# A DeltaNet and SwiGLU kernel's prologue: beta through TensorE, L in three operations, conversions after the rounds

## Chip, cores, metric

One core of a Trainium2 chip runs the whole program. The metric is device time of one execution in microseconds (us). Engine names as the profile has them: PE is TensorE (PEld its weight loads), DVE is VectorE, ACT is ScalarE, POOL is GpSimd, SP is SyncE, which here only issues DMAs.

## The reference

Two blocks follow each other, all in float32. The first is a gated linear attention with a delta rule, for 4 batches and 8 heads, 768 steps, head size 48:

```python
k_n = k / (np.linalg.norm(k, axis=-1, keepdims=True) + 1e-06)
for t in range(S):
    y[t] = q[t] @ state
    v_old = state.T @ k_n[t]
    state = state + beta[t] * outer(k_n[t], v[t] - v_old)
```

Its output, as 3072 tokens of 384 features, goes through a feed-forward block with d_ff 1536: `(silu(x @ w_gate) * (x @ w_val)) @ w_out`.

## The kernel before

The attention is done in chunks of 64 steps (12 chunks; c is the chunk). In a chunk, the recurrence becomes a triangular system: K times K transposed (the "gram"), scaled by beta and by the norms of K, is inverted, and the inverse is multiplied with V. PE does the products; DVE does the substitution, since it is a chain of small steps. Two chunks form a group g, and 32 heads of batch and head lie side by side in the tiles. The feed-forward products of a chunk (lines L1093, L1189, L1216, L1299) fill PE between the attention's steps, and they make up most of the time.

The order of the instructions on each engine is written out by hand (a manual schedule): each engine works its own queue strictly in that order, and waits by semaphore for what an instruction needs. The change touches only the start of the program, before PE has feed-forward work. In that start, in order:

- SP and ACT each issue one half of the loads of chunk 0's K, then of chunk 1's (`load_k`, L135). Rows of 48 floats make many small packets. Then 16 small loads of beta (`load_beta`, L387) go out, alternately from POOL and from SP or ACT; each brings eight rows for one block of 32 steps, so that beta arrives in the layout in which it is used. SP goes on with Q of chunk 0, K of 2 and 3, Q of 1, V and the weights (`stage`, L253).
- `unread` (L582): 100 small products on PE whose result nobody reads, before K has landed.
- `norms` (L363, L371) on DVE: squares of K and their sums; the square root on POOL (L375).
- `turned` (L444): eight transposes on PE per K or Q, copied out by ACT (L446). K has 16 heads in two banks of one PSUM tile, called p_t.
- `first_gram` (L592, L593) for chunks 0 and 1: for every head two products, one for the upper ("hi") 32 steps with 32 columns, one for the lower ("lo") 32 steps with 64 columns. `first_diag` (L598) copies the diagonal blocks out, one half by ACT, one by DVE. ACT copies beta to `beta_b` (L1573). DVE turns the blocks (L1577), scales them (L621), and `first_substitution` (L637, L643) does 15 steps of inversion for 16 by 16 blocks. `first_z` turns the result back, and `spread_z` (L656, L658) writes it to `ztp`.
- `low_copies` (L605, L610) on ACT: the parts L of the gram below the diagonal blocks, in six operations per chunk, three per half of the partitions.
- Q's and later K's transposes, and the grams of chunks 2 and 3 and of Q with K (`gram_steps`, L458), on PE behind that.
- `n_products` (L667): L times the block inverse, on PE; then `advance(0)`, which holds a short series: the product p_u (L876), and three rounds of two half rounds each, a product on PE (L896) and an addition on DVE (`plus`, L1260). Then p_y, the copies y, the transposes to `x_ffn` (L989, L992), and the first gate product (L1189).

The weights come as float32 and are split into parts by `power_step` on ACT (L265, L271) and `convert` on DVE (L282, L290, L302), piece by piece. Pieces 0, 2, 4 are the first columns of the gate weights; 1, 3, 5 of the value weights. Before, one conversion stands behind each half round of chunk 0:

```python
        for n in (0, 2, 4, 1, 3, 5):
            step("advance", advance, 0)
            converts_first(n)
```

Of the kernel before, what the change touches and what calls it, by code (L numbers as in the profile page):

```python
# [8 lines left out]
FP32 = mybir.dt.float32  # L9
# [4 lines left out]
C = 64  # L14
DP = 64
R = 32
# [4 lines left out]
def kernel(  # L21
# [25 lines left out]
    nc = tc.nc  # L47

    B, H, S, D = q.shape
# [63 lines left out]
    ident = const.tile([128, 128], FP32, name="ident")  # L113
    nc.gpsimd.memset(knp[0][:, :, :, D:DP], 0.0)
    make_identity(nc, ident)
    for t in knp[1:] + qpad:
        nc.gpsimd.memset(t[:, :, :, D:DP], 0.0)
    ZB = 2
    ztp = [const.tile([128, 2, HH, C], FP32, name=f"zt{i}") for i in range(ZB)]
# [103 lines left out]
    place_of += [("z1", H_ * n) for n in (2, 3, 1, 0)]  # L223
    place_of += in_wo + in_work + (in_z1 + in_work) * 3

    beta_s = places["wo"].bitcast(FP32)[:, 6 * H_ : 6 * H_ + NG * 128]
    LATE = {"zb": 18, "p_sb": 12}
    freed_by = {}
    for n, (name, lo) in enumerate(place_of):
# [27 lines left out]
    def power_step(n):  # L257
        if n in powers or n not in staged:
            return
        dst, _, t, f0, m = pieces[n]  # L260
        power = words(hp[10 + (n // 2 % 4 if n < N_HALF else (0, 2, 3, 1)[(n + 2) % 4])])
        power = power[:, n % 2 * m : n % 2 * m + m] if n < N_HALF else power[:, 0:m]
        powers[n] = power
        words_of = staged[n].rearrange("p (f two) -> p f two", two=2)
        nc.scalar.activation(  # L265
            dst[:, t, f0 : f0 + m],
            words_of[:, :, 1].bitcast(FP32),
            ACTF.Copy,
            scale=2.0**-112,
        )  # L270
        nc.scalar.activation(power, words_of[:, :, 0], ACTF.Copy, scale=2.0**-29)  # L271
# [75 lines left out]
    def every():  # L347
        for bp in range(NB):
            for j in range(NJ):
                for n, (par, b) in enumerate(ORDER):  # L350
                    yield bp, j, par, b, bp == 0 and j == 0
# [28 lines left out]
                out=beta_b[:, g], in0=beta_b[:, g], in1=r_n, op=ALU.mult  # L380
            )

    def load_beta(at, queue=nc.gpsimd):

        s_, blk, c, par = at // 8, at // 4 % 2, at // 2 % 2, at % 2
        lo, m = 64 * c + R * blk, (NG - 1) * 128 + R
        queue.dma_start(  # L387
            out=beta_s[8 * at : 8 * at + 8, 0:m],
            in_=beta.rearrange("(b bp) (j par) s -> b par bp j s", b=2, par=2)[
                s_ ^ par, par, :, :, lo : lo + m  # L390
            ],
        )

    def first_n():
        n = n_t[0].rearrange("p c h -> p (c h)")
# [17 lines left out]
    def banks(name, tag):  # L413

        if type(tag) is int:
            return [ps_ffn([128, 512], name, tag + i) for i in range(2)]
        p = ps_pair(name, tag)
        return [p[:, 0], p[:, 1]]

    def turned(c, of_q, tag=None):  # L420

        if tag is None:
            tag = "py" if of_q else "px"
        x = qpad[c % QB] if of_q else kn_of(c)
        if of_q:
            xt = work.tile([128, NB * NJ * 2 * C], FP32, name="qt", bufs=1)
        else:
            xt = kt_of(c)
        if c >= blocks_of[of_q][1]:
            xt_v = xt.rearrange("p (b bp j i) -> p bp j b i", bp=NB, b=2, j=NJ)  # L430
            (qt if of_q else kt)[c] = xt_v
            blocks = blocks_of[of_q][2]
            nc.vector.transpose(xt, blocks.rearrange("p bp h d -> p (bp h d)"))
            spent.append(1.8)
            if c + 1 < NCH:
                late_loads.append(lambda: load_blocks(of_q, c + 1))
            return
        xt = xt.rearrange("p (bp j b i) -> p bp j b i", bp=NB, j=NJ, b=2)
        (qt if of_q else kt)[c] = xt
        p_t = banks("p_t", tag)  # L440
        for bp in range(NB):
            for j in range(NJ):
                at = slice(128 * j, 128 * j + 128)
                nc.tensor.transpose(p_t[bp][:, at], x[:, bp, 2 * j : 2 * j + 2], ident)  # L444
        for bp in range(NB):
            nc.scalar.copy(xt[:, bp].rearrange("p j b i -> p (j b i)"), p_t[bp])  # L446
        if of_q and c + QB < Q_BLOCKS:
            load_q(c + QB)
# [104 lines left out]
    def first_tiles():  # L553
        a = work.tile([128, C * 2 * HH], FP32, name="a_sb")
        for c in range(2):
            l_sb[c] = a[:, R * R * c : R * R * (c + 1)].rearrange(
                "p (h k) -> p h k", k=C
            )
        first_of["flat"] = new_mb().rearrange("p k i -> p (k i)")
        first_of["diag"] = first_of["flat"].rearrange("p (j h) -> p h j", j=R)  # L560
        first_of["zb"] = places["z1"].bitcast(FP32)[:, 4 * H_ - 1056 : 4 * H_]
        first_of["mb"] = places["wo"].bitcast(FP32)[:, 2 * H_ : 2 * H_ + 1056]
        nc.vector.memset(first_of["zb"], 0.0)
        nc.vector.memset(a, 0.0)
        for x, rows in enumerate((slice(16, C), slice(R, C), slice(48, C), slice(0, R))):
            nc.vector.tensor_reduce(
                out=m_two[:, x],
                in_=ident.rearrange("p (b n) -> p b n", b=2)[:, :, rows],
                axis=mybir.AxisListType.X,
                op=ALU.add,  # L570
            )
        nc.vector.tensor_tensor(
            out=m_rows, in0=m_two[:, :, 0], in1=m_two[:, :, 1], op=ALU.add
        )
        nc.vector.tensor_scalar_mul(m_low, m_rows[:, 0:3], -1.0)

    def unread():

        p = ps_pair("p_t", "px")[:, 0]
        for n in range(100):  # L580
            q_ = QUADS[n % 4][0]
            nc.tensor.matmul(p[q_, 0:1], ident[q_, q_], ident[q_, 0:1])  # L582

    def first_gram(c, tag):

        p_g = ps_pair("p_g", tag)
        p_v = p_g.rearrange("p par (x h i) -> p par x h i", x=2, i=R)
        for bp, j, par, b, _ in every():
            k_v = kt[c][half_of(par), bp, j, b].rearrange("p (x i) -> p x i", x=2)
            h, s_ = NJ * bp + j, b ^ par  # L590
            hi, lo = slice(64 * s_, 64 * s_ + R), slice(64 * s_ + R, 64 * s_ + C)
            nc.tensor.matmul(p_v[hi, par, 1, h], k_v[:, 0], k_v[:, 0])  # L592
            nc.tensor.matmul(p_v[lo, par, :, h], k_v[:, 1], k_v)  # L593
        return p_v

# [3 lines left out]

    def low_copies(c, p):  # L600
        l_v = l_sb[c].rearrange("p (par h) k -> p par h k", par=2)
        for s_ in range(2):
            hi, lo = QUADS[2 * s_][0], QUADS[2 * s_ + 1][0]
            for rows, x in ((hi, 0), (lo, 2)):
                nc.scalar.mul(  # L605
                    l_v[rows, :, :, B16 * x : B16 * x + B16],
                    p[rows, :, 1, :, 0:B16],
                    m_low[rows, x : x + 1],
                )
            nc.scalar.mul(l_v[lo, :, :, 0:R], p[lo, :, 0], -1.0)  # L610

    def first_scale(r_b):
        zb, b = first_of["zb"], beta_b[:, 0]
# [46 lines left out]
    def n_products(c, p_n, pars):  # L660

        zt = ztp[0][:, c]
        p_v = [p.rearrange("p (bp j i) -> p bp j i", bp=NB, j=NJ) for p in p_n]
        for bp, j, par, b, _ in every():
            if par in pars:
                rows, h = half_of(b ^ par), HH // 2 * par + NJ * bp + j
                nc.tensor.matmul(  # L667
                    p_v[par][half_of(b), bp, j], l_sb[c][rows, h], zt[rows, h]
                )
# [732 lines left out]
    def converts_first(*ns):  # L1402

        convert(list(ns), 0)
        for n in ns:
            todo.remove(n)
# [132 lines left out]
    with tc.manual_schedule(  # L1539
# [6 lines left out]
        }  # L1546
    ):
        new_n(0)
        for at in range(0, 16, 2):
            load_beta(at)  # L1550
            load_beta(at + 1, nc.sync if at % 4 else nc.scalar)
        first_tiles()
        norms(0)

        norms(1)
        load_q(0)
        load_k(2)
# [8 lines left out]
        copy_a, copy_v = nc.scalar.copy, nc.vector.tensor_copy  # L1566
        unread()
        turned(0, False)
        turned(1, False, "py")
        p_g = [first_gram(0, "px"), first_gram(1, "py")]  # L1570
        first_diag(0, 0, p_g[0], copy_a)
        first_diag(0, 1, p_g[0], copy_v)
        copy_a(beta_b, beta_s.rearrange("p (g r) -> p g r", g=NG)[:, :, 0:R])  # L1573
        first_diag(1, 0, p_g[1], copy_a)
        r_b = first_n()
        first_diag(1, 1, p_g[1], copy_v)
# [32 lines left out]
        power_step(2)  # L1609
        for x in range(2):  # L1610
            spread_z(1, x, nc.scalar)
            power_step((4, 1)[x])
        power_step(3)
        power_step(5)
        for n in (0, 2, 4, 1, 3, 5):
            step("advance", advance, 0)
            converts_first(n)
        step("advance", advance, 0)
        p_n = banks("p_n", "px")
        n_products(1, p_n, (0,))  # L1620
        step("advance", advance, 0)
        n_products(1, p_n, (1,))
        scale_v(1)
        for par in range(2):
            n_copy(1, p_n, par)
# [73 lines left out]
```

## Time and profile before

| | |
|---|---|
| median of 3 runs | 711.52 us (709.63 to 712.78) |
| the profiled execution | 709.14 us |
| its span, first to last instruction | 707.4 us |
| PE busy | 683.2 us, 97% of the span |
| PEld busy | 643.0 us, 91% |
| DVE busy | 473.6 us, 67% |
| ACT busy | 261.8 us, 37% |
| POOL busy | 52.9 us, 7% |
| mean granted clock of PE | 0.992 |

The shares are averages over very different stretches. In the page's slices, each character is one fortieth of the span (17.7 us) and gives the busy tenths; the first three slices are the start that the change touches. A row of the order of time reads: start, duration, engine, line, operation, output and inputs, shapes, count, and in brackets the idle time before and what ended it. "issue" stands for waiting for nothing that the profile shows. A row of the chain reads start, duration, what; a row of the waits reads who waited for whom, the sum, how often, the longest.

### The profile page before, as it was taken

What the parts mean: (1) busy time and instruction counts of PE and PEld (TensorE: products, weight loads), DVE (VectorE), ACT (ScalarE), POOL (GpSimd) and SP (SyncE); (2) the same over time, 40 slices, a digit from 0 to 9 for tenths busy, and PEclk for the clock granted to TensorE, in tenths of its full rate; (3) what the DMA queues carried; (4) which work ended last, traced back from release to release, by engine and by line L of the source; (5) the groups of instructions that cost most, each with busy time, mean ns of one, the idle gap of its engine ahead of it and who ended that gap; (6) DMA issues with size and microseconds to landing.
All of it is one profiled execution on the core that took longest, in us unless ns stands there. A gap on an engine that the chain in (4) does not pass through costs nothing.

```text
span 707.4 us, 25711 instructions
## 1 busy us (share of the span) xinstructions
PE 683.2 (97%) x11440; PEld 643.0 (91%) x11440; DVE 473.6 (67%) x1092; ACT 261.8 (37%) x548; POOL 52.9 (7%) x46
## 2 busy tenths in 40 slices
PE   6689999999999999999999999999999999999997
PEld 5578888856899999999999999999999999999997
DVE  6775689797899857988458788379855345333342
ACT  3657686302543433335233235133153132132230
POOL 7000021205000030000200000300000000000000
PEclk9799999999999999999999999999999999999999
DMA  8982717004652332265234175144142142221210
GB/s 131 244 218 54 212 46 224 1 23 81 192 101 60 77 85 70 71 112 113 63 74 93 30 138 106 26 113 93 41 104 63 27 96 61 53 63 46 68 45 23
DMA packets 144111, 62.57 MB, mean 88 GB/s; under 512 B 123136, under 2 KB 126208, under 8 KB 144000
## 3 DMA queue, kind: packets, MB, share of 16 engines
q1 hardware_dynamic: 141600, 60.27, 36.4%
q8 instruction: 90, 1.47, 0.9%
q10 hardware_dynamic: 2144, 0.48, 0.5%
q0 software_dynamic: 256, 0.17, 0.1%
q14 instruction: 21, 0.17, 0.1%
HBM read 53.82 MB, written 7.08 MB: 86 GB/s over the span
## 4 chain that ended last, share of the span: by engine, by line
PE 91%; DVE 3%; ACT 2%; issue 2%; DMA 1%; SPq 0%; DVEq 0%; ACTq 0%
PE ffn L1093 42%; PE ffn L1299 19%; PE ffn L1189 8%; PE ffn L1216 4%; PE p_g L458 3%; PE p_u L876 2%; PE p_s L944 2%; PE p_r L838 2%; PE p_y L932 1%; PE p_y L847 1%; DMA kn<-in_k_dram 1%; PE p_f L989 1%; PE p_u L896 1%; PE p_t L444 1%; PE p_j L801 1%
## 5 line engine op out<-in xcount | busy, mean ns | idle before, releaser
L1093 PE MATMUL ffn<-x_ffn,wg_sb 128*128 128x128 f32 x840 | 128.3, 275 | 0.4 <-ACT x_ffn L992 0.2
L1093 PE MATMUL ffn<-x_ffn,wv_sb 128*128 128x128 f32 x840 | 128.1, 275 | 0.0
L1093 PEld LDWEIGHTS ffn<-x_ffn,wg_sb 128*128 128x128 f32 x840 | 111.1, 192 | 0.7 <-ACT ffn L1149 0.3
L1093 PEld LDWEIGHTS ffn<-x_ffn,wv_sb 128*128 128x128 f32 x840 | 110.7, 192 | 0.0
L1123 ACT ACTIVATE sil<-ffn 128x256 f32<-128x256 f32 x120 | 46.0, 383 | 132.7 <-PE ffn L1093 128.0
L1299 PE MATMUL ffn<-wo_sb,h_f 128*128 128x192 f32 x480 | 83.4, 327 | 0.0
L1128 DVE TENSOR_TENSOR h_f<-sil,ffn 128x256 f32<-128x256 f32 x120 | 49.6, 418 | 48.4 <-ACT sil L1123 46.1
L1299 PEld LDWEIGHTS ffn<-wo_sb,h_f 128*128 128x128 f32 x480 | 78.1, 190 | 0.4
L1260 DVE TENSOR_TENSOR ffn<-ffn,p_sb 128x512 f32<-128x512 f32 x58 | 40.4, 697 | 44.3 <-ACT ffn L1149 43.2
L1093 PE MATMUL ffn<-x_t,h_f 128*128 128x128 f32 x480 | 61.1, 280 | 0.2 <-ACT ffn L1106 0.2
L1093 PEld LDWEIGHTS ffn<-x_t,h_f 128*128 128x128 f32 x480 | 56.2, 191 | 1.4 <-ACT ffn L1106 0.4
L536 DVE TENSOR_TENSOR zb<-zb,tmp 128x31 f32<-128x31 f32 (+15 forms) x155 | 53.1, 343 | 5.3
L746 POOL TENSOR_TENSOR n_b<-mb,half 128x32 f32<-128x32 f32 x5 | 30.0, 6002 | 344.8 <-DVE mb L500 344.8
L530 DVE TENSOR_TENSOR tmp<-zb,mb 128x31 f32<-128x31 f32 (+15 forms) x155 | 52.7, 340 | 4.0
L1260 DVE TENSOR_TENSOR o_sb<-o_sb,ffn 128x192 f32<-128x192 f32 x49 | 17.2, 352 | 51.2 <-PE ffn L1299 49.1
L1106 ACT COPY ffn<-ffn 128x512 f32<-128x512 f32 x30 | 17.1, 572 | 63.7 <-PE ffn L1093 57.3
L1299 PE MATMUL ffn<-last_k,h_f 128*128 128x192 f32 x200 | 35.9, 327 | 0.0
L1189 PE MATMUL ffn<-x_ffn,wg_sb 128*128 128x256 f32 x144 | 34.3, 384 | 0.0
L1189 PE MATMUL ffn<-x_ffn,wv_sb 128*128 128x256 f32 x144 | 33.8, 382 | 0.0
L1299 PEld LDWEIGHTS ffn<-last_k,h_f 128*128 128x128 f32 x200 | 32.9, 190 | 0.0
L1093 PE MATMUL ffn<-x_ffn,p_sb 128*128 128x128 f32 x216 | 30.3, 283 | 0.5 <-issue 0.5
L1189 PEld LDWEIGHTS ffn<-x_ffn,wv_sb 128*128 128x128 f32 x144 | 27.0, 190 | 3.7
(267 smaller groups left out, 1073.5 us busy)
## 6 DMA issues: line engine op xcount, KB each, us to landing
h_f<-w_s SPq DMA_DIRECT2D x60, 256.0 KB, 3.1
p_sb<-w_s SPq DMA_DIRECT2D x27, 256.0 KB, 2.7
vin<-in_v_dram SPq DMA_DIRECT2D x48, 96.0 KB, 3.1
out_dram<-o_sb SPq DMA_DIRECT2D x48, 96.0 KB, 2.3
kn<-in_k_dram SPq DMA_DIRECT2D x20, 192.0 KB, 4.6
zt<-in_moe_w_out_dram SPq DMA_DIRECT2D x6, 384.0 KB
qpad<-in_q_dram SPq DMA_DIRECT2D x36, 64.0 KB, 2.8
w_s<-h_f SPq DMA_DIRECT2D x7, 256.0 KB, 3.7
```

The costliest lines, as they stand in the source:

```text
L458: nc.tensor.matmul(p_v[par][half_of(b if of_q else b ^ par), bp, j], kt[c][half_of(par), bp, j, b], xt[half_of(par), bp, j, b],)
L530: nc.vector.tensor_tensor(out=t_v, in0=zb[:, 0 : j + 1, j : j + 1].to_broadcast([128, j + 1, m]), in1=mb[:, j : j + 1, j + 1 : R].to_broad ...
L536: nc.vector.tensor_tensor(out=zb[:, 0 : j + 1, j + 1 : R], in0=zb[:, 0 : j + 1, j + 1 : R], in1=t_v, op=ALU.add,)
L746: nc.gpsimd.tensor_tensor(out=n, in0=mb.rearrange("p j i -> p (j i)")[:, 0 : R * R : R + 1], in1=half, op=ALU.pow,)
L1093: nc.tensor.matmul(p[:, u], w(u), moving, start=start and u == 0, stop=True, skip_group_check=True,)
L1106: nc.scalar.copy(p_y, p_x)
L1123: nc.scalar.activation(sil[:, n].rearrange("p (i n) -> p i n", i=2), p[:, 0:2], ACTF.Silu)
L1128: nc.vector.tensor_tensor(out=h_of(c, f, j), in0=sil[:, n].rearrange("p (i n) -> p i n", i=2), in1=p[:, 2:4], op=ALU.mult,)
L1189: nc.tensor.matmul(ps[name][:, i], w_sb[:, t, (f + i) * 128 : (f + i + 1) * 128], xts[c][:, t], start=(t == 0 and i == 0), stop=(t == KT - 1),
L1216: nc.tensor.matmul(p_o, hs[c, f - f % 2][:, f % 2, bp * 128 : (bp + 1) * 128], wo_sb[:, f], start=(f == 0), stop=(f == FT - 1),)
L1260: nc.vector.tensor_tensor(out=out, in0=a, in1=b, op=ALU.add)
L1299: nc.tensor.matmul(p[x, part], a(f - f % 2)[:, f % 2], b(f), start=not begun and f == 0, stop=f == FH - 1, skip_group_check=True,)
```

## The change

- Beta is loaded by four loads from POOL alone, into 16 rows in each of two places (`beta_rows`). Eight PE products with parts of the identity (`spread_beta`) put it into PSUM in the layout in which it is used, and ACT copies it to `beta_b`.
- PE's order becomes: first K's transposes, its gram, the beta products, second K's transposes, its gram. Before, both transposes stood ahead of both grams.
- The hi products get the same 32 columns twice (64 columns), so that L's parts lie alike on all partitions; `low_copies` takes three operations on 128 partitions per chunk. The rest of L's tile is zeroed by two smaller memsets.
- `unread` makes 88 products of `half` instead of 100 of `ident`.
- The zeroing of the pad of chunk 0's Q moves from POOL to DVE, between the norms of the first and of the second K.
- ACT does both `spread_z` of chunk 1 ahead of the power steps 4, 1, 3, 5; the six half rounds stand without conversions between them; conversions 0 and 2 follow the rounds, 4 follows the copies of y, and 1, 3 and 5 come after the second `n_products` in the order.

```diff
-    for t in knp[1:] + qpad:
+    for t in knp[1:] + qpad[1:]:
         nc.gpsimd.memset(t[:, :, :, D:DP], 0.0)
...
+    def beta_rows(s_):
+        return slice(32 + 64 * s_, 48 + 64 * s_)
+
+    def load_beta():
+        for s_ in range(2):
+            for par in range(2):
+                at = beta_rows(s_).start + 8 * par
+                nc.gpsimd.dma_start(
+                    out=beta_s[at : at + 8],
+                    in_=beta.rearrange(
+                        "(b bp) (j par) s -> b par (bp j) s", b=2, par=2
+                    )[s_ ^ par, par],
+                )
+
+    def spread_beta(copy):
+        p = ps_ffn([128, NG * R], "p_b", 0)
+        x = beta_s.rearrange("p (g c blk r) -> p g c blk r", g=NG, c=2, blk=2)
+        for s_ in range(2):
+            rows = beta_rows(s_)
+            for blk in range(2):
+                for c in range(2):
+                    lanes = slice(rows.start - 16 * c, rows.start - 16 * c + R)
+                    nc.tensor.matmul(
+                        p[QUADS[2 * s_ + blk][0]],
+                        ident[rows, lanes],
+                        x[rows, :, c, blk],
+                        start=c == 0,
+                        stop=c == 1,
+                    )
+        copy(beta_b.rearrange("p g r -> p (g r)"), p)
...
-        nc.vector.memset(a, 0.0)
+        for c in range(2):
+            nc.vector.memset(l_sb[c][:, :, 48:C], 0.0)
...
-        for n in range(100):
+        for n in range(88):
             q_ = QUADS[n % 4][0]
-            nc.tensor.matmul(p[q_, 0:1], ident[q_, q_], ident[q_, 0:1])
+            nc.tensor.matmul(p[q_, 0:1], half[q_], half[q_, 0:1])
...
-            nc.tensor.matmul(p_v[hi, par, 1, h], k_v[:, 0], k_v[:, 0])
+            twice = k_v[:, 0:1].to_broadcast([half_rows, 2, R])
+            nc.tensor.matmul(p_v[hi, par, :, h], k_v[:, 0], twice)
...
-        for s_ in range(2):
-            hi, lo = QUADS[2 * s_][0], QUADS[2 * s_ + 1][0]
-            for rows, x in ((hi, 0), (lo, 2)):
-                nc.scalar.mul(
-                    l_v[rows, :, :, B16 * x : B16 * x + B16],
-                    p[rows, :, 1, :, 0:B16],
-                    m_low[rows, x : x + 1],
-                )
-            nc.scalar.mul(l_v[lo, :, :, 0:R], p[lo, :, 0], -1.0)
+        for x in range(3):
+            nc.scalar.mul(
+                l_v[:, :, :, B16 * x : B16 * x + B16],
+                p[:, :, x // 2, :, B16 * (x % 2) : B16 * (x % 2) + B16],
+                m_low[:, x : x + 1],
+            )
...
-        for at in range(0, 16, 2):
-            load_beta(at)
-            load_beta(at + 1, nc.sync if at % 4 else nc.scalar)
+        load_beta()
         first_tiles()
         norms(0)
+        nc.vector.memset(qpad[0][:, :, :, D:DP], 0.0)
         norms(1)
...
         turned(0, False)
-        turned(1, False, "py")
-        p_g = [first_gram(0, "px"), first_gram(1, "py")]
+        p_g = [first_gram(0, "px")]
+        spread_beta(copy_a)
         first_diag(0, 0, p_g[0], copy_a)
         first_diag(0, 1, p_g[0], copy_v)
-        copy_a(beta_b, beta_s.rearrange("p (g r) -> p g r", g=NG)[:, :, 0:R])
+        turned(1, False, "py")
+        p_g.append(first_gram(1, "py"))
...
             spread_z(1, x, nc.scalar)
-            power_step((4, 1)[x])
-        power_step(3)
-        power_step(5)
-        for n in (0, 2, 4, 1, 3, 5):
+        for n in (4, 1, 3, 5):
+            power_step(n)
+        for _ in range(6):
             step("advance", advance, 0)
-            converts_first(n)
+        converts_first(0, 2)
         step("advance", advance, 0)
+        converts_first(4)
         p_n = banks("p_n", "px")
         n_products(1, p_n, (0,))
         step("advance", advance, 0)
         n_products(1, p_n, (1,))
+        converts_first(1, 3)
+        converts_first(5)
         scale_v(1)
```

More of the change, by code (lines that the diff above doesn't have):

```diff
@@ L224 @@
     place_of += in_wo + in_work + (in_z1 + in_work) * 3
-    beta_s = places["wo"].bitcast(FP32)[:, 6 * H_ : 6 * H_ + NG * 128]
+    beta_s = places["wo"].bitcast(FP32)[:, 6 * H_ : 6 * H_ + S]
     LATE = {"zb": 18, "p_sb": 12}
@@ L381, in divide_beta @@
             )
[L383 to L391, printed above, removed]
-        )
+    def beta_rows(s_):
[26 more added lines that the diff above has]
+        copy(beta_b.rearrange("p g r -> p (g r)"), p)
     def first_n():
@@ L587, in first_gram @@
         p_v = p_g.rearrange("p par (x h i) -> p par x h i", x=2, i=R)
+        half_rows = C
         for bp, j, par, b, _ in every():
@@ L601, in low_copies @@
         l_v = l_sb[c].rearrange("p (par h) k -> p par h k", par=2)
-        for s_ in range(2):
-            hi, lo = QUADS[2 * s_][0], QUADS[2 * s_ + 1][0]
-            for rows, x in ((hi, 0), (lo, 2)):
-                nc.scalar.mul(
-                    l_v[rows, :, :, B16 * x : B16 * x + B16],
-                    p[rows, :, 1, :, 0:B16],
-                    m_low[rows, x : x + 1],
-                )
-            nc.scalar.mul(l_v[lo, :, :, 0:R], p[lo, :, 0], -1.0)
+        for x in range(3):
[4 more added lines that the diff above has]
+            )
     def first_scale(r_b):
```

## The prediction

> **What bounds it.** I read the page's slices first: TensorE (PE) is full from the third slice on, so the change can only act in the first 53 us, before the first gate product (L1189, 53.39 us).
>
> ```profile
> PE   6689999999999999999999999999999999999997
> PEclk9799999999999999999999999999999999999999
> DMA  8982717004652332265234175144142142221210
> ```
>
> From 53.4 us on PE is busy 645.6 of 653.6 us (busy time by windows): what moves that first product moves the end, nearly one for one. Next the chain of waits and the order of time, for what ends last before it.
>
> ```profile
> ACT kt L446 <- DMA wo_sb<-in_beta_dram: 5.5, 1, 5.5
> SPq L135 <- DMA kn<-in_k_dram: 3.0, 1, 3.0
> ...
> 5.85 1.94 PE L444 MATMUL p_t<-ident,kn 128*128 128x128 f32 x8 [1.11 <-DMA kn<-in_k_dram]
> 9.17 1.94 PE L444 MATMUL p_t<-ident,kn 128*128 128x128 f32 x8 [1.39 <-DMA kn<-in_k_dram]
> 9.32 1.07 ACT L446 COPY kt<-p_t 128x512 f32<-128x512 f32 x2 [5.54 <-DMA wo_sb<-in_beta_dram]
> 11.15 1.07 ACT L446 COPY kt<-p_t 128x512 f32<-128x512 f32 x2 [0.76 <-PE p_t L444]
> 19.59 1.09 PE L444 MATMUL p_t<-ident,kn 128*128 128x128 f32 x8 [0.58 <-ACT a_sb L610]
> ```
>
> The first row: ACT copies the first K only at 9.32, because it is still issuing its beta loads; the transposes had ended at 7.79. The second copy starts when all eight of its transposes are done (11.11). The last row: eight transposes took 1.09 at 19.59 against 1.94 here, and 1.97 at 23.57, where the windows grant 0.50; so I read the first 17 us as half clock, though the clock row says 1.00.
>
> ```profile
> 29.44 0.52 PE ffn L458 x33
> 29.95 4.41 issue
> 34.36 1.02 PE ffn L458 x28
> 35.38 0.01 PE p_n L667
> 35.39 0.10 PE ffn L458 x3
> 35.49 1.71 PE p_n L667 x62
> ```
>
> PE stops for 4.41 us in the midst of one product group (second Q), on nothing the profile names. The inverse that p_n needs was ready at 31.40 (end of ACT L656, 30.66 + 0.74). So p_n began 4.1 late. The instruction queue carries 90 packets of 16 KB for PE's 22,880 records (two each per matmul), 254 a packet; one of them starts at 31.99, between weight packets, and PE resumes 2.4 later. I take this as PE out of instructions behind weight traffic.
>
> ```profile
> 40.62 0.56 DVE L1260 TENSOR_TENSOR uu<-v,ffn 128x384 f32<-128x384 f32 x1 [0.64 <-PE ffn L896]
> 41.09 0.29 DVE L282 TENSOR_SCALAR h_f<-wg_sb 128x256 uint32<-128x256 uint32 x1
> 41.41 0.42 DVE L290 SCALAR_TENSOR_TENSOR wg_sb<-wg_sb,h_f 128x256 uint32<-128x256 uint32 x1
> 41.87 0.43 DVE L302 CUSTOM_DVE_ANT_0 wg_sb<-wg_sb,h_f 128x512 uint16<-128x512 uint16 x1
> 42.21 0.55 DVE L1260 TENSOR_TENSOR uu<-v,ffn 128x384 f32<-128x384 f32 x1
> ```
>
> The rounds beat at DVE's pace: one plus and one conversion, 1.59 us (40.62 to 42.21), where PE's half round takes 1.04 (64 records of L896 in 2.07).
>
> **Part by part,** on the profiled execution's own clock (span 707.4, execution 709.14; the median of the three runs is 711.52, so 2.4 is added at the end).
>
> *Beta loads.* Of 16 loads, 4 leave SP, 4 ACT and 4 POOL. ACT is free for the first K's copies: 7.83 to 8.90 instead of 9.32 to 10.39. POOL issues its fourth by 5.4 (2.6, then after the selects three by 0.52), in front of its pow at 8.64. A load landed 4.3 to 6.3 after its issue (beta's own rows), so the last is in by 9.7 to 11.7; PE needs the first two at 11.0, the others a little later. I take no wait; bound 0 to 0.7.
>
> *PE's new order.* Gram 0 no longer stands behind the second K's transposes, but those now stand behind gram 0 and the eight beta products, and their copies are covered by nothing (beta's copy, 0.35 by L1573, and the first diagonal's 0.6 stand before them on ACT, beside the transposes). From the first K's landing (5.85): transposes 1.94, copies 1.11 (with the handoff), gram 0 2.1 (11.04 to 13.19), beta products b, transposes 1.5 (between 1.09 and 1.94), copies 1.11, gram 1 2.0 (14.27 to 16.27).
> The wider hi product of each pair (64 columns for 32) costs nothing if the lo product beside it, already 64 wide, sets the pace; 128 records in 2.0 us is 16 ns each where one lasts 239 to 311, so many are in flight. Bound 0 to 1.4 (by 64 for 48 columns would be 0.7, doubled for the half clock); I take 0.
> b: eight products are 16 records of 192 columns. The only 192-column row, L1299, spends 83.4/480 = 174 ns a record at full clock, 348 at half. One after another: 2.8 or 5.6. They lie on four tiles of the array, four records each; side by side 0.7 or 1.4. The second-Q group (64 records on four tiles in 1.90 at half clock, 30 ns each, for 64 columns; 192-column rows scaled give 116) shows about four abreast, but there neighbours change tile with every product, here only with every second. I take b = 2.5, between, with both ends kept.
> The Trainium skill, "TensorE: Matmul & The Clock Gate", Part 3, says that a weight load overlaps a running matmul only in another row group; here each row group gets four products in a row. By that rule b would be at its upper end and the whole gain 0.6; the gram rows, with hi and lo on one row group, speak for more overlap than the rule allows.
> Sum: gram 1 ends at 5.85 + 1.94 + 1.11 + 2.1 + 2.5 + 1.5 + 1.11 + 2.0 = 18.1, against 16.27: 1.8 later (from 0.4 earlier to 7.5 later, with all bounds).
>
> *From gram 1 to p_n.* The diagonal's copies, the turn, 15 substitution steps and the spread stay: 16.27 to 31.40, 15.13. So p_n can begin at 33.3. L in three operations: before, per K, four at 0.466 and two at 0.572, 3.0 of ACT; now three at 0.466, 1.4. That is 3.2 off ACT between 16.7 and 23.5, where PE's third and fourth transposes waited for it (19.59 and 23.57), so the second-Q group comes earlier behind gram 1 (about 9.8 instead of 29.27 - 16.27 = 13.0). A block's packet is asked for when the block before it is begun; counting 256 records a block back from the stop, that took 3.2 us (11.05 to 14.27, where PE also idled 1.08) to 6.5 (27.9 to 34.36). Here it is asked for in the third K's gram, at about 26.5: PE goes on at 29.7 to 33.0, before or at 33.3. The stall is spent beside the substitution. P moves from 35.49 to 33.3: gain 2.2.
> The Trainium skill, "Runtime: NRT & Kernel Launch", Instruction fetch mechanics, has blocks of 256 instructions and calls a crossing mostly hidden. The 4.41 row says not here; were the stall something else that keeps p_n 19.2 behind gram 1 (35.49 - 16.27), P would be 37.3 and the sum 4.0 worse.
>
> *Conversions behind the rounds.* DVE leaves the beat: six half rounds at PE's 1.04 are 6.24, then p_y two by 1.04. The y copies on DVE stand behind the plus (to R + 6.95) and conversions 0 and 2 (1.85, as for two pieces at 70.58): R + 8.8 against p_y's end R + 8.3, so 0.5 is paid, and y ends at R + 9.95, against 51.77 - 39.43 = 12.34. Gain 2.4. The other four conversions (1.2, 1.85, 1.2) and scale_v (0.96) then run after y for 5.2, in DVE's 4.81 idle plus the 0.96 that scale_v had: queued behind them are the next conversions (58.24) and the vin subtraction (59.79, y + 8.0); both fit. Pieces 1, 3, 5 are wanted by L1189 at y + 7.7. If that cover fails, each piece costs 1.2. No staging load hangs on these six.
> PE now runs the rounds without gaps: instruction blocks last 4.2 instead of 6.4 us. With 4.4 from crossing to resume (38.16 to 43.36 was 5.2) I allow 0.3 (0 to 2). After the shift, p_n no longer starts where the clock came back at 37.83 before the rounds; half clock may reach into them: 0.6 (0 to 2).
>
> *Q and later K.* In the built program Q's load waits for nothing: the memset writes columns 48 to 63, the load 0 to 47. So Q is asked for at about 2.6 instead of 9.05, where SP waited for K. SP's ring still serves K before Q; the loads lead by 2 to 3 us, beside DVE and PE work: 0. Had it waited for the squares, 8.8: also 0. The memset itself is 0.3 on DVE before the second K's squares (8.8 against landing 9.04): hidden, else 0.3 beside a norm chain with 3 us to spare.
>
> *Edits at nothing:* half the memset of L (DVE idle before 5.82), 12 fewer idle products, begun at 1.05 with `half` instead of 1.90 with `ident` (done by 3.6, first K at 5.85; a gain of 0.85 if that warmed the clock, which 2.84 of them did not).
>
> Sum: 2.2 + 2.4 - 0.9 = 3.7. 709.14 - 3.7 = 705.4, on the median 707.8.
>
> **Rivals.**
> 1. *Beta products abreast, clock up early:* b = 0.7, transposes 1.09: gram 1 at 15.9, P 31.0, no allowances: gain 6.9, 704.6. For it: four tiles. Against: PE's idle at 7.8 to 8.9 keeps the clock low.
> 2. *The packet still ends last, or the rounds run cold:* P near 35, gain 1.5, 710.0. For it: weights, 3 us earlier, flow from about 21 to 30, through the crossing.
> 3. *Slower: beta lands late.* SP's ring no longer pauses from 6 to 9 us but keeps 192-byte packets of Q and K on all engines, beside POOL's. PE stands in order before the beta products, with the second K behind it. Each us of landing after 11.1 costs one us; from 14.8 on the kernel is slower than before, from 18.4 by over 0.5%. With products one after another at half clock those points fall to 11.7 and 15.3. Landing at 14 with these: 713.8. Against: landings of 4.3 to 6.3 after issue, with as many packets on the rings.
>
> **Numbers.** Forecast 707.8 (707 to 709.5): 0.44. Rival 1: 0.21. Rival 2: 0.21. Rival 3: 0.14. 0.5%, about what a measurement of this kernel can tell from no change, is 3.6 us: faster below 707.9, slower above 715.1. The forecast lies on the lower line: 0.25 of it faster, 0.19 same; rival 1 faster; rival 2 same; of rival 3 0.08 slower. Faster 0.46, same 0.46, slower 0.08. Range 704.2 to 712.5: rival 1 in, the worst of rival 3 out.
>
> **What would show it.** Kt copy at 7.8; the beta products' length; gram 1's end at 18.1; the second-Q group done before the spread; plus after plus every 1.04; first L1189 near 49.7. Gram 1 later than 21.9 makes the whole wrong; a stall over 2 us in the rounds makes the third part wrong.

## The result: no change that can be measured

Twelve runs of the changed kernel have a median of 710.08 us (706.26 to 712.61). Twelve runs of the kernel before, with the three already shown among them, have 709.85 (708.11 to 712.78). The ratio is 0.9995, 95% interval 0.9974 to 1.0016. A second set (e7 below) gave 0.9985 (0.9969 to 1.0001). By the two ratios the change gains 0.4 and 1.1 us, where 3.7 were forecast. The time lies in the stated range (704.2 to 712.5), 2.3 above the forecast's value, and above the 707 to 709.5 that the forecast itself was given.

The profiled execution took 710.49, span 708.8. The start first, in order of time on ACT (start, duration, what it waited for):

```profile
7.77 1.07 ACT L467 COPY kt<-p_t 128x512 f32<-128x512 f32 x2 [4.00 <-PE p_t L465]
...
15.37 1.07 ACT L467 COPY kt<-p_t 128x512 f32<-128x512 f32 x2 [1.08 <-PE p_t L465]
```

The first K's copies are at 7.77 instead of 9.32; ACT waits for the transposes, not for its own loads. The second K's copies moved from 11.15 to 15.37. Groups on PE, 5 to 19 us (count, then busy time, mean ns of one, idle before and its releaser):

```profile
L616 PE MATMUL p_g<-kt 64*32 64x64 f32 x128 | 4.1, 310 | 2.3 <-ACT kt L467 2.3
...
L406 PE MATMUL ffn<-wo_sb,ident 16*32 16x192 f32 x16 | 2.0, 518 | 0.4 <-DMA wo_sb<-in_beta_dram 0.4
```

Both grams now wait for their copies (2.3 for the two), and the beta products take 2.0, behind 0.4 of waiting for beta. Gram 1 ends at 18.56; before it was 16.27. Now the chain that ended last, from the spread to y:

```profile
31.94 0.79 ACT zt L677
32.73 0.06 issue
32.79 2.23 PE p_n L688 x62
35.02 1.03 PE p_u L897 x36
36.05 1.70 issue
37.75 0.62 PE p_u L897 x25
...
38.92 8.44 PE ffn L917 x230
47.36 0.41 issue
```

p_n starts at 32.79 instead of 35.49, straight behind ACT's spread: the inverse now sets it. The second-Q group's stall is still there, but beside the substitution (PE's waits, 26 to 50 us: total, times, longest):

```profile
PE ffn L479 <- issue: 2.7, 1, 2.7
```

But of the 2.70 gained at p_n, 2.19 are gone by the rounds, for PE stops 1.70 in the midst of p_u, again on nothing that the profile names. (By the chain p_n took 2.23 here and 1.71 before; but before, its first records ran from 35.08, beside the last of the second-Q group. Counted from there it took 2.12, and half clock is granted to p_n in both.) The rounds start at 38.92 for 39.43. Their pluses on DVE:

```profile
40.56 0.56 DVE L1281 TENSOR_TENSOR uu<-v,ffn 128x384 f32<-128x384 f32 x1 [1.10 <-PE ffn L917]
42.27 0.55 DVE L1281 TENSOR_TENSOR uu<-v,ffn 128x384 f32<-128x384 f32 x1 [1.15 <-PE ffn L917]
43.52 0.56 DVE L1281 TENSOR_TENSOR uu<-v,ffn 128x384 f32<-128x384 f32 x1 [0.70 <-PE ffn L917]
44.45 0.56 DVE L1281 TENSOR_TENSOR uu<-v,ffn 128x384 f32<-128x384 f32 x1 [0.38 <-PE ffn L917]
```

DVE now waits for PE. The first pluses are 1.71 and 1.25 apart, while half clock is granted (39.38 to 42.79), the later ones 0.93. y ends at 50.19, 11.27 behind the rounds' start (before: 12.34). The copy of the state, which ends the chunk, starts at 54.51 for 56.09: 1.58 gained. It is lost again, and 1.4 more, around 255 us, where PE stops 2.00 before L1114 and then gets half clock from 257.83 to 261.25. The page's row of that group has the stop:

```profile
L1114 PE MATMUL ffn<-x_ffn,p_sb 128*128 128x128 f32 x216 | 30.5, 285 | 2.0 <-issue 2.0
```

### The profile page after: what moved, and what is told of

It is laid out like the page before. It is cut to its first block, busy times and chain, and to the rows that moved or that the text cites. A ratio compares the mean times of both kernels' runs of the same rounds, so it can differ in the third digit from the quotient of the medians.

```text
span 708.8 us, 25670 instructions
## 1 busy us (share of the span) xinstructions
PE 685.9 (97%) x11432; PEld 645.8 (91%) x11432; DVE 472.2 (67%) x1094; ACT 258.0 (36%) x542; POOL 50.6 (7%) x41
## 4 chain that ended last, share of the span: by engine, by line
PE 91%; DVE 3%; ACT 2%; issue 1%; DMA 1%; POOL 0%; DVEq 0%; ACTq 0%; POOLq 0%
PE ffn L1114 42%; PE ffn L1320 19%; PE ffn L1210 8%; PE ffn L1237 4%; PE p_g L479 3%; PE p_u L897 2%; PE p_s L965 2%; PE p_r L859 2%; PE p_y L868 1%; PE p_y L953 1%; PE ffn L917 1%; DMA wo_sb<-in_beta_dram 1%; PE p_f L1010 1%; PE p_u L917 1%; PE p_j L822 1%
## 5 line engine op out<-in xcount | busy, mean ns | idle before, releaser
L1114 PE MATMUL ffn<-x_ffn,wg_sb 128*128 128x128 f32 x840 | 129.2, 277 | 0.3 <-ACT x_ffn L1013 0.2
L1114 PE MATMUL ffn<-x_ffn,wv_sb 128*128 128x128 f32 x840 | 128.6, 276 | 0.0
L1114 PEld LDWEIGHTS ffn<-x_ffn,wg_sb 128*128 128x128 f32 x840 | 112.0, 193 | 0.6 <-ACT ffn L1170 0.3
L1114 PEld LDWEIGHTS ffn<-x_ffn,wv_sb 128*128 128x128 f32 x840 | 111.2, 193 | 0.0
L1114 PE MATMUL ffn<-x_t,h_f 128*128 128x128 f32 x480 | 61.1, 280 | 0.2 <-ACT ffn L1127 0.2
L1114 PEld LDWEIGHTS ffn<-x_t,h_f 128*128 128x128 f32 x480 | 56.2, 192 | 1.4 <-ACT ffn L1127 0.4
L1114 PE MATMUL ffn<-x_ffn,p_sb 128*128 128x128 f32 x216 | 30.5, 285 | 2.0 <-issue 2.0
```

What stands on the lines that cost most here:

```text
L1114: nc.tensor.matmul(p[:, u], w(u), moving, start=start and u == 0, stop=True, skip_group_check=True,)
```

## The experiments

Three marks are read from every trace: the start of the rounds, the end of y and the start of chunk 0's state copy. "Ratio" is to runs of the kernel before on the same chip, with its 95% interval. A number of a product, as in "product 728", is here and in the expectations its place among PE's MATMUL records in the trace; one of the program's fp32 products other than a transpose makes two such records. Counted so, the stalls of 2.7 and 1.70 stand before products 728 and 855, and in the kernel before those of 4.41 and 0.93 before 729 and 984. The distances are 127 and 255: one and two times 128, to one record, and 128 records with their weight loads are 256 instructions, a packet of the instruction queue. So the first theory: PE runs out of instructions at every 128th record. The packets agree: those of 16 KB that come before the two stalls end at 29.24 and 36.11, and PE goes on 1.35 and 1.64 later; in the kernel before, one ends at 33.03 and PE goes on 1.33 later.

**Blocks moved by the count: e1_idle70.**

```
-        for n in range(88):
+        for n in range(70):
```

> The changed kernel with 70 unread products at the start in place of 88, and nothing else. Theory: TensorE's issue stalls (2.7 in the second-Q group, 1.70 in p_u, 2.00 in the products behind p_j<-t,z at 257.35) come from instruction blocks of 128 products that are crossed at a fixed count, and a block is there 4.8 to 7.2 us after the one before it was entered while weights flow, about 3.2 later. 18 products fewer move every crossing 18 products on: the hidden stall sits at product 746 instead of 728, the one in p_u at product 874 instead of 856 and shorter (0 to 1.4 for 1.70), and the one behind p_j falls among products of 300 ns each and is gone, with the half clock after it (2.0 + 0.6). Profile: y end 48.8 to 50.2, span about 705.5 (704.5 to 707) against 708.8; median 2 to 4 us below the changed kernel. Rival (the stalls are chance of one execution, or sit at a place in time): they stay in p_u and behind p_j or move without order, and the time is that of the changed kernel, 710.1. Second rival (the unread products keep the clock up): the time is slower than 710.1.

Measured: 705.55, ratio 0.9967 (0.9947 to 0.9986); span 702.7. Eighteen idle products are 36 records, so the blocks cut the work 36 records further on, and not 18 as I had it. The second-Q group and p_u have no stall (0.8 stands in a gram of K, 0.6 in the next p_n); PE's longest wait from 10 to 62 us is for the inverse:

```profile
PE p_n L688 <- ACT zt L677: 3.7, 1, 3.7
```

Rounds start at 37.35, y ends at 48.77, state copy 53.31 (54.51), and nothing over 0.35 is lost near 255 us. Taking out eighteen products that do no work gains more (0.2 to 0.3%) than the whole change, by the medians of the ratios; their intervals overlap. The stalls are gone from both places, as the theory has it. Half clock up to 42.14 cost 1.4 between the first three pluses (1.71 and 1.51 for 0.93).

**The conversions' move, undone in the changed kernel (e3) and done alone in the kernel before (e5).**

```
-        for _ in range(6):
-            step("advance", advance, 0)
-        converts_first(0, 2)
+        for n in (0, 2, 4, 1, 3, 5):
+            step("advance", advance, 0)
+            converts_first(n)
```

> The changed kernel with the six first conversions back between the half rounds, one behind each. My recorded step priced their move at 2.4. In the changed kernel's profile the rounds ran at 1.71 a plus at first (half clock) and met 0.4 of issue, and y ended 11.27 behind the start of the rounds where 9.95 was forecast. Theory now: the move is worth only what the half clock and the instruction blocks leave of it, 1.0 (0.5 to 1.5): y ends 12.0 to 12.4 behind the start of the rounds, the first gate product 0.5 to 1.5 later, 711 in the median. Rival (the move is worth its full 2.4): 712.5. Rival (DVE's work is only put behind y and paid there): no difference, 710.1.

Measured: 707.98, ratio 0.9993 (0.9978 to 1.0008). y ends 12.58 behind the rounds' start, state copy 55.68, which is 1.17 later than in the changed kernel.

> The kernel before with only the conversions moved behind the half rounds. The recorded step: the rounds lose 2.4 (y at 49.4 instead of 51.77), 2.4 faster than the kernel before. Theory now: the rounds of the kernel before run at full clock, but two instruction blocks are crossed in them at 5.2 us each (38.17, 43.36, then 48.5), which leaves 1.3 to 2.0: y at 49.8 to 50.5, 708.2 in the median where the kernel before has 709.85. Rival (paid back behind y by DVE): the first gate product no earlier than 53.2, no difference.

Measured: 707.10, ratio 0.9984 (0.9965 to 1.0002). y ends 11.54 behind the rounds' start (12.34 before), state copy 54.94: 1.15 earlier. In these executions the move is worth 1.2 at the chunk's end both ways, where half clock and blocks leave it. The size is loose, for two executions of the changed kernel differ by 1.84 at that mark (e7), and none of these ratios tells the kernels apart. The 2.4 without allowances was not reached in either; "paid back behind y" is refuted: from y's end to the state copy it is 4.32 before and 4.32 after.

**The beta products beside the copies: e4_beta_behind.**

```
         p_g = [first_gram(0, "px")]
+        turned(1, False, "py")
         spread_beta(copy_a)
         first_diag(0, 0, p_g[0], copy_a)
         first_diag(0, 1, p_g[0], copy_v)
-        turned(1, False, "py")
```

> The changed kernel with the beta products and their copy behind the second K's transposes instead of ahead of them. Theory: of gram 1's delay against the kernel before (18.55 for 16.27), 1.1 to 1.5 is the copies of the second K that nothing covers, plus the 0.43 wait for beta; with the beta products (2.05) beside these copies gram 1 ends at 16.9 to 17.2, p_n starts at 31.3 to 31.7 instead of 32.79, unless the second-Q group (its stall ended 30.6) still holds it, and the first gate product comes 1.0 to 1.6 earlier; time 708.5 to 709.2 in the median. Rival (the instruction blocks take it back in p_u and the rounds): gram 1 earlier by 1.5 but y's end by less than 0.5, 710.1. Rival (the beta products run one after another wherever they stand, and their transposes gain nothing): gram 1 at 18.5.

Measured: 705.13, ratio 0.9955 (0.9939 to 0.9971). Gram 1 ends at 16.22, state copy 51.70 (54.51), both better than expected. The groups on PE, 5 to 17 us:

```profile
L616 PE MATMUL p_g<-kt 64*32 64x64 f32 x128 | 4.1, 310 | 1.2 <-ACT kt L467 1.2
...
L406 PE MATMUL ffn<-wo_sb,ident 16*32 16x192 f32 x16 | 1.5, 520 | 0.0
```

One of the two waits for copies is gone, and the wait for beta; the products take 1.5. So the place of eight products cost the change 2.3 us at gram 1. Blocks still cost: 0.89 in p_u, then 0.52 in the rounds and 1.42 in y.

**Beta as before: e10_beta_as_before.** The change with the 16 loads of before, both K's transposes ahead of both grams, no beta products.

```
-        load_beta()
+        for at in range(0, 16, 2):
+            load_beta(at)
+            load_beta(at + 1, nc.sync if at % 4 else nc.scalar)
...
-        spread_beta(copy_a)
+        copy_a(beta_b, beta_s.rearrange("p (g r) -> p g r", g=NG)[:, :, 0:R])
```

> The changed kernel with beta as before: 16 loads spread over SP, ACT and POOL, no beta products, both K's transposes ahead of both grams; L in three and the conversions behind the rounds stay. My recorded step: the beta part makes gram 1 1.8 later (2.3 in the profile). Theory: without it gram 1 ends at 16.3 again, product 600 is crossed 1 to 2 earlier, p_n starts at 31.0 to 32.0 in place of 32.8, and the chunk's end comes 0.8 to 1.6 earlier than in the changed kernel; 0.996 to 0.998 of the kernel before. So the beta part alone would be a loss as it is placed. Rival (the instruction blocks hold p_n anyway, so that an earlier gram 1 is worth nothing): as the changed kernel, 0.998 to 1.000. Rival (ACT's loads cost more than the beta products): slower than the changed kernel, above 1.000.

Measured, 6 runs: 706.25, ratio 0.9942 (0.9919 to 0.9964), below what either theory gave, and on the side of "the beta part alone is a loss". Its profile does not show how: gram 1 ended at 18.25, since a block came 3.06 late in it (product 349; 0.84 in e5, 1.08 before), p_n started at 32.54 behind a second-Q stall of 4.73, and the state copy came at 53.00. By the times the beta part as placed costs; by this one execution it does not. It also has 16 records fewer, so that the blocks cut other products; what such a shift is worth by itself (e1, e13) is not separated from it. That stays open, beside e4, where trace and time agree.

**L in six again: e9_l_in_six.**

```
-        for x in range(3):
-            nc.scalar.mul(
-                l_v[:, :, :, B16 * x : B16 * x + B16], ...
+        for s_ in range(2):
+            hi, lo = QUADS[2 * s_][0], QUADS[2 * s_ + 1][0]
+            ...
```

> The changed kernel with L's low copies in six operations of quarters a chunk again (and the whole of L cleared), all else as changed. My recorded step: L in three takes 3.2 of ACT out of 16.7 to 23.5, so that the second-Q group and its block stall move beside the substitution and p_n is free 2.2 earlier. Theory: with six, product 600 is crossed at 27.3 to 28.2 instead of 25.8, the stall ends at 32.5 to 34.5, p_n starts at 33.5 to 35 for 32.8, y ends 0.5 to 2 later; time 1 to 2 slower than the changed kernel of the same call. Rival (the substitution alone sets p_n): p_n at 32.8, no difference.

Measured: 708.03, ratio 1.0011 (0.9992 to 1.0030); the changed kernel run beside it 706.81, 0.9985. Product 600 came at 28.22, the stall ended at 34.23, p_n started at 34.93, all inside the expectation; the state copy at 57.48 is 3.0 later (4.8 later than in e7), more than expected, for the next block stands in p_u:

```profile
PE ffn L479 <- issue: 3.9, 1, 3.9
...
PE p_u L899 <- issue: 2.4, 1, 2.4
```

L in three is thus the part that frees p_n, as the prediction had it: 2.1 us there.

**The changed kernel once more: e7_changed_again.**

> The changed kernel itself, once more beside the others on one chip. Theory: the 2.00 of issue at 257.35 and the half clock behind it were this one execution's, not the program's (with the conversions put back, which leaves every instruction count as it was, the same place took 0.69 and no half clock); this profile will show less than 1.2 there, the p_u stall at product 855 (0.9 to 1.9), and the stall at 728 (2.5 to 3.1) again. Time 0.999 of the kernel before (0.997 to 1.001), 707.9 for 708.6. Rival (the stall is the program's): 2.0 again at the same place.

Measured: 706.81, ratio 0.9985 (0.9969 to 1.0001). In the profiled execution (704.62, the lowest of its twelve) the chain reads:

```profile
32.83 2.22 PE p_n L688 x62
35.05 1.03 PE p_u L897 x36
36.08 0.34 issue
36.42 0.62 PE p_u L897 x25
...
44.97 0.92 issue
```

The same products stall, by other amounts: 4.2 for 2.7 in the second-Q group (again hidden), 0.34 for 1.70 in p_u, 1.13 for 2.00 at 252 us and no half clock behind it. The first two are outside what I expected, the last inside. So the place of a stall belongs to the program, and its length differs from execution to execution; the state copy comes at 52.67 here, at 54.51 there.

**Weights out of the way: e6_weights_later,** on e4.

```
-        for n in range(14, 18):
-            stage(n)
         first_z()
-        for n in range(18, 23):
-            stage(n)
...
         converts_first(0, 2)
+        behind = const.tile([1, 8], FP32, name="behind")
+        nc.sync.dma_start(out=behind, in_=wg_sb[0:1, 0, 0:8])
+        for n in range(14, 23):
+            stage(n)
```

> The kernel of e4_beta_behind, with the loads of weight pieces 14 to 22 asked for behind the first converted piece (about 44 us, through a small load that reads it) in place of 31 to 42 us. Theory: an instruction block takes 4.9 to 6.9 us from crossing to resume in 27 to 45 us because weights fill the DMA engines there (share 0.8 to 1.1), against 3.0 to 3.3 where nothing loads. With the rings quieter from 35 us on, the two stalls at products 982 (0.52) and 1110 (1.42) go or fall below 0.3 each; the one in p_u (0.89), whose block is asked for at 27.7, stays. y ends 1.2 to 2.0 earlier than the 45.91 of e4_beta_behind; median 703.5 (702.5 to 704.5) for a kernel before of 708.6. Rival (blocks take that long by themselves): stalls and time as in e4_beta_behind, 705.1. Rival on the slow side (pieces 14 to 19, wanted from 58 us on, come late, or the loads hit the next chunk's blocks): 706 or more.

Measured: 708.85, ratio 1.0007 (0.9990 to 1.0024), the slow rival. PE's waits, 10 to 62 us:

```profile
PE ffn L479 <- issue: 4.4, 1, 4.4
PE p_y L868 <- issue: 2.7, 1, 2.7
```

(The 45.91 of the expectations of e6 and e8 is the end of p_y's last product in e4; y's end there, by the mark used here, is 47.38.) Of the stalls of 0.52 and 1.42 none is left, and 0.7 stays in p_u, as the theory had it, though half clock up to 43.3 also made the rounds ask for fewer products. But 2.7 appears at 56.6, just behind the moved loads, and 4.4 in the second-Q group, ahead of the edit. That weights make blocks late fits this run, and it is not settled by it.

**Both gains together: e8_beta_idle70.** e4 with 70 idle products.

> The kernel of e4_beta_behind with 70 unread products in place of 88. Theory: the two gains lie in different stretches, gram 1 two us earlier from the one, blocks crossed at better places from the other, and add in part: rounds start at 34.8 to 35.8, y ends 0.5 to 1.5 before the 45.91 of e4_beta_behind, and the 1.6 at product 2894 moves or shrinks; median 704.0 (702.5 to 705.2) for a kernel before of 708.6. Rival (blocks are entered no faster, so that a stall taken away at one count comes back at the next): as e4_beta_behind, 705.1.

Measured, 6 runs: 702.50, ratio 0.9917 (0.9895 to 0.9940). Rounds start at 34.89, y ends at 45.86 (47.38 in e4), state copy 51.39. It beats the kernel before by 0.8%, and the changed kernel run beside it (706.81) by 0.6%. e1 and e4 were 0.33% and 0.45% under before: within the intervals, of 0.2% either way, the two add.

**Is the shift's gain the change's? e13_before_idle82.** The kernel before, `range(100)` made `range(82)`.

> The kernel before with 82 unread products in place of 100, nothing else: the shift of 18 that gave the changed kernel 0.3% (0.9967 for 0.9985 to 0.9995). Theory: what the shift is worth depends on which products the blocks then cut, not on the change; here the 4.41 in the second-Q group moves to product 747 of that group and ends at 33 to 34.6, p_n starts 0 to 2 earlier than 35.49, and the stalls of 0.88 at 257 and 0.53 at 354 move; 0.997 to 1.000 of the kernel before. Rival (fewer unread products help by themselves, through queue or clock): the full 0.3% here too, with the second-Q stall at its old product. Rival (the start's clock suffers): slower than 1.000.

Measured, 7 runs: 705.53, ratio 0.9945 (0.9925 to 0.9966): more than expected, and no part of the change is in it. The profiled execution (707.62, above its median) shows the 4.41 gone from the second-Q group, 1.1 at p_n and 2.9 at the rounds' start instead (36 records on, as in e1), and the state copy at 56.57. Which block the median owes its gain to is open; later than 240 us the stalls of 0.88 and 0.53 are gone.

**The clock, or the blocks? e12 and e14.** On e8, with 75 and 76 idle products at the start for 70, wide idle products ahead of p_n, to keep the clock up.

```
+        p_wide = ps_pair("p_wide", "px")[:, 0]
+        for _ in range(9):
+            nc.tensor.matmul(p_wide, ident, kts[0][:, 0:512])
```

> The kernel of e8_beta_idle70 with nine unread products of 512 columns ahead of p_n, where TensorE waited 5.0 us for the inverse, and 75 unread products at the start, so that the block that was crossed at p_n's first product is crossed among the nine. Theory: they keep the clock up (in e8_beta_idle70 half clock was granted from 27.5 to 34.3, and p_n and p_u took 1.82 and 2.09 for 64 products each, 28 to 33 ns one), so p_n and p_u take 0.95 to 1.2 each, and the block is entered near 28 instead of 30.9, so that the next one is there at 33 to 34 instead of 36.0: rounds start at 33.0 to 34.2 for 34.89, y ends 1 to 2.5 earlier; later the blocks fall as in e4_beta_behind, which may cost 0.5 to 2 (175 us, 254 us). Median 0.5 to 1.5 below e8_beta_idle70, 0.990 of the kernel before. Rival (the blocks alone set the pace from 25 to 46 us, the clock is hidden behind them): p_n and p_u shorter, but a stall of the same length behind them, y as in e8_beta_idle70. Rival (nine products at half clock last 8 us and hold p_n up): p_n later than 31.5, slower.

Measured: 708.79, ratio 0.9984 (0.9966 to 1.0001), the last rival. I had taken a product for one record; it is two:

```profile
L1613 PE MATMUL p_wide<-kt,ident 128*128 128x512 f32 x18 | 9.9, 700 | 2.3 <-issue 2.3
```

They held p_n to 37.17. What followed ran warm: p_n 0.98, p_u 1.10, the half rounds 0.93 but for one of 1.14.

> The kernel of e12_wide_products with four wide products in place of nine and 76 unread products in place of 75. In e12 a wide product showed as two records of 0.43 at full clock and 0.86 to 0.93 at half, so that nine lasted from 28.07 to 37.17 and held p_n up; but p_n and p_u then took 0.98 and 1.10 (1.82 and 2.09 in e8_beta_idle70), and all six half rounds ran at 0.93. Theory: the four are done at 30 to 31, the block that e8_beta_idle70 enters at 30.9 is entered inside them at 28 to 29.5, p_n starts at 30.4 to 31.3 with the clock up, the rounds start 2.8 behind it as in e12 (33.2 to 34.3, against 34.89), y ends 10.8 behind that (44.0 to 45.1, against 45.86), the state copy comes at 49.6 to 50.8 for 51.39; behind it the blocks fall as in e4_beta_behind, worth 0 to 2 against e8_beta_idle70. 0.989 to 0.993 of the kernel before. Rival (blocks, not the clock, pace everything up to the rounds): p_n and p_u short again, but an issue stall of 1 to 2.5 at the rounds' start or in them, y no earlier than 45.8. Rival (half clock in the four, as the stall among them lets it fall): p_n later than 31.5, and no gain.

Measured, 10 runs: 702.81, ratio 0.9929 (0.9908 to 0.9950), no better than e8. The chain:

```profile
26.05 3.25 issue
...
29.51 3.63 PE p_wide L1613 x8
33.14 1.14 PE p_n L688 x64
...
39.49 0.53 issue
40.02 3.90 PE ffn L917 x126
43.92 1.48 issue
```

p_n starts 2.7 later than in e8 and the rounds 0.96 later, at full clock throughout (granted 1.00 from 17.74 to 700). Yet the blocks that begin at about products 982 and 1110 of each count start at 40.02 and 45.39, in e8 at 40.58 and 45.96, and the state copy comes at 51.73 for 51.39. So from the second-Q group to y the instruction blocks set the pace: neither a warm clock nor 2.7 us at p_n moves the chunk's end by more than 0.6. (The 6.8 us of e12 do: its state copy came at 55.04.)

## Why the prediction was right and wrong

*Beta loads:* right in what they cost. The first K was copied at 7.77 (forecast 7.8), and PE waited 0.43 for beta (bound 0 to 0.7). The landing was not: a load took 6.9 to 7.4 from its issue, where 4.3 to 6.3 were taken over from before, and the last was in at 11.81 (forecast 9.7 to 11.7). PE needed only the first two at once, and they were in at 11.26.

*Beta products:* b was 2.05, forecast 2.5 between 0.7 and 5.6. Sixteen records of 518 ns in 2.05 are four abreast. The rule of the Trainium skill ("TensorE: Matmul & The Clock Gate", Part 3), as the prediction read it, would have put b at 5.6; the measurement decides against that reading. The wider hi products cost nothing (gram 0 8.90 to 10.96).

*Gram 1* at 18.56 for 18.1: right, with terms that cancel. Beta's products were 0.45 short, the wait of 0.43 was not in the sum, and the second K's transposes took 1.9 for 1.5. *p_n* at 32.79 and 32.83 for 33.3: right, with the stall beside the substitution as forecast, and e9 shows that L in three does it.

*From p_n to the rounds* is the step that failed. "The stall is spent beside the substitution. P moves from 35.49 to 33.3: gain 2.2" booked p_n's gain as the rounds' gain, carrying the 3.94 from p_n to the rounds over from before. It measured 6.13, and 4.77 in e7. The stall ends at 30.59, and I read the traces so that the next block is asked for only then; p_u needs it 128 records later. From the first record of one block to that of the next took 7.16 there (4.3 to 7.2 over all kernels wherever PE stalled between 22 and 49 us), and p_n and p_u reach the next block's first record in 5.5. In the kernel before, that block was there in 3.81, without a stall. What differs most is when the next block's packet starts: 4.59 behind the first record of the block that PE is in, 1.93 in e7, 1.25 in the kernel before. The DMA share in these three stretches was 0.99, 0.49 and 1.16, so the load alone does not explain it. Rival 2 had this cause ("the packet still ends last") and its price, a gain of 1.5 and 710.0, but looked for it at p_n, which it put near 35.

*Conversions:* right in sum, in part by luck. y ended 11.27 and 10.72 behind the rounds' start, forecast 9.95 + 0.9. The half clock's term was too small (1.6 in the first execution, about 0 in e7, for 0.6), as was the blocks' (0.4 and 1.4 for 0.3); but the rest took 9.3 for 9.95, for a half round at full clock took 0.93 where 1.04 was read from before. That the four conversions behind y fit was right to 0.01 (4.32 from y's end to the state copy in both kernels).

*Edits at nothing:* 12 idle products fewer and eight beta products more leave 8 records less in front of p_n, so the blocks cut the work 8 records further on. What that is worth was not tried; a shift of 36 changed the time by 0.2 to 0.55% (e1, e8, e13).

*Q and later K:* Q was asked for at 2.58, without a wait. It was not tried alone.

At chunk 0's end the two executions had gained 1.58 and 3.42, forecast 3.7. From there to the end of the span, the kernel before takes 651.3, the changed one 654.3 and 650.2. The Trainium skill ("Runtime: NRT & Kernel Launch", Instruction fetch mechanics) calls a crossing of blocks mostly hidden. Here single crossings cost up to 4.7 us of PE's time, and their length differs between executions of one program. The forecast used the row of 4.41 once, for the stall it could see, and not for the stall that would come next.

Why the ratios give 0.4 and 1.1 and not the 1.6 to 3.4 of the two profiles is not settled: the runs spread over 4 to 6 us, and e7's profile is the lowest of its set. That the time fell into the stated range says little for the sum: the range took in rival 1 and most of rival 3.

## What to carry to other kernels

An "issue" idle that the profile puts down to nothing, and that recurs at distances of 128 MATMUL records (256 instructions with their weight loads), fits a late instruction block: count records to the next multiple, and ask what the engine does there, before a gain on the near side is booked. Small added products belong where the engine already waits: here the same eight cost 2.3 us in front of a copy and nothing beside it. And where a start full of short products runs beside a stream of loads, try the cheapest edit first, the number of idle products at the start; it gave 0.2 to 0.55% on three versions (each known to about 0.2%), with no part of the change under study in one of them.

## What the runs showed of the hardware that I had not expected

Where PE stalled between 22 and 49 us, the gap between two blocks' first records was 4.3 to 7.2 us (in the changed kernel, with a DMA share of 0.9 to 1.05 from 20 to 46 us). At 254 us it was 3.3 (product 4292 at 254.06, 4420 at 257.35; DMA share 0.06 between them). The same stall of the same program took 2.00 and 1.13 in two executions, and 0.69 in e3, whose PE program is the same. The stalls at these block bounds between 22 and 62 us ended 1.3 to 1.9 us behind the end of a 16 KB packet of the instruction queue. A product of 128 x 512 fp32 elements shows as two records, which start 0.43 apart at full clock and 0.85 at half. In e8 PE was idle from 25.35, and half clock was granted from 27.5 to 34.3, into p_n and p_u; yet e14, without it, ended no earlier.
